# A lower pace for the weight loads, logits turned ahead of the expert products, and a new opening list

## The chip, the cores and the metric

One core of a Trainium2 chip. The time is device microseconds for one execution of the whole program, as the median of a few runs. The names of the engines are those of the profile: PE (TensorE matmuls, with PEld for its weight loads), DVE (VectorE), ACT (ScalarE), POOL (GpSimd) and SP (SyncE, which here issues almost all the DMAs).

## What is computed

A banded attention, a soft mixture of experts and a two-layer FFN with tanh-shrink, one behind the other, all in float32. Cut to what matters:

```python
# attention: 4 batches, 8 heads, 512 local and 32 global positions, head size 64
out_g = sm(scale * q_g @ k_all.T) @ v_all            # the global rows see everything
s_ll  = where(|i - j| <= 32, scale * q_l @ k_l.T, -1e9)
out_l = sm(concat(scale * q_l @ k_g.T, s_ll)) @ concat(v_g, v_l)
x = concat(out_g, out_l)                             # 2304 tokens x 512

# soft mixture of 8 experts with 4 slots each
logits = x @ phi                                     # 2304 x 32
d = softmax of logits over the tokens;  c = softmax of logits over the slots
slot_out[e] = relu((d.T @ x)[e] @ w1[e]) @ w2[e]     # 512 -> 1024 -> 512
x = c @ slot_out

# FFN
h = x @ w_in;  g = h - tanh(h);  out = g @ w_out     # 512 -> 2048 -> 512
```

## The kernel before

The program is scheduled by hand: the order in which the code calls an engine's operations is the order in which that engine runs them. It has four stages.

**Attention** (to about 126 us of the profiled execution) runs 33 iterations over pieces of the sequence. PE computes scores, transposes and products with the values, DVE and ACT the softmax, POOL spreads q and k and rolls v. Meanwhile SP loads the next q, k and v, and also prefetches what later stages need: the expert weights, in pieces of 512 KB that go to free buffers called slot (and later to buffers of attention as they come free: k_w, v_w, q, pg), and the FFN's w_in. How many go in an iteration is set by one line in the loop:

```python
while queued < LEAD + PACE * it:
```

`queued` counts the KB of everything loaded so far, so that an iteration with few loads of its own gets more weights. Behind the last iteration the weights go out as fast as buffers come free and the DMA queue takes them. All of this stands at line 124, a helper. At most a handful of loads are under way at a time: before it issues the next, SP waits for an older one.

**The hand-over** (to about 137 us) ends the softmax over the tokens and forms the slots' inputs. Line 906 turns a column of maxima, 854 turns the slots' inputs into the PSUM bank `sit`, and DVE's 930 copies it to the two halves of `siT`, on which the expert products rest. Three small DVE operations behind it (`d3["sums"]`, line 399; 935; `make_irep`, 828) prepare the sums by which the expert outputs are scaled.

**The expert stage** (to about 171.5 us) runs 16 units, `UNITS`, each an expert's W1 (line 1026) or W2 (line 1065) in two halves. In between stand the transposes of the hidden layer (1049) and the combine weights, c, in five pieces, of 4, 4, 4, 4 and 1 tiles of 128 tokens: `combine(4 * k, ..)` turns the logits `lT` (lines 972 and 974) and computes a softmax on DVE and ACT, and `combine_turn` turns the result back (998) and casts it into place (ACT, 1000 and 1011). `CPREP` and `CTURN` say behind which units these stand. The stage's last work is the conversion of w_out's first chunk from a 64-bit form: head (ACT, 562), shift, high and low (DVE, 566, 571, 576), whi (ACT, 1091) and wlo (POOL, 1092).

**The FFN** follows. Its beginning is written out as a list of words, `OPENING`, that are called one by one: `sos` scales and copies the experts' outputs (ACT, 1312), `turn` and `soT` transpose them (1318), `m0`, `rows`, `ms`, `parts`, `mhi` and `mlo` form the product of the experts' outputs with w_in block by block (1327, 1140, 1154, 1158, 1162), `head`, `S`, `H`, `L`, `whi` and `wlo` convert the chunks of w_out. `h:i:part` is the hidden product of step i (1197), `sq`, `t0`, `t1`, `hi` and `lo` its activation and its split into a high and a low half (ACT 1201, DVE 1207 and 1211, ACT 1219, POOL 1223), and `T:i:j` three products of 512 columns (1236, 1237, 1238) into the accumulator of tile j; the third needs `lo`. From step 9 a loop does the same in a fixed pattern, up to about 382 us.

`keep_warm(bank, n)` (line 674) is a product of n columns whose result nobody reads; one of 256 columns stands before ahead of `sos`.

Of the kernel before, what the change touches and what calls it, by code (L numbers as in the profile page):

```python
# [12 lines left out]
ALU = mybir.AluOpType  # L13
# [5 lines left out]
NT = 17  # L19
NE = 8  # L20
WARM = 3
LEAD, PACE = 2700, 1200
KEEP = 2
SPK = 1
C0 = 4
# [24 lines left out]

PHASES = [(0, 6, 0, 8), (6, 6, 0, 8), (12, 5, 0, 8), (0, 6, 8, 16), (6, 6, 8, 16), (12, 5, 8, 16)]
OPENING = """
    sos:0 turn:0 sos:1 turn:1 turn:2 head:1 S:1 turn:3 soT:1 H:1 L:1 soT:0 m0:0 head:2 m0:1 m0:2 m0:3 mhi:0 mlo:0
    rows:1 ms:1 S:2 whi:1 wlo:1 h:0:2 sq:0:2 h:0:3 t0:0:2 t1:0:2 h:0:1 sq:0:3 t0:0:3 t1:0:3 sq:0:1 parts:1 mhi:1
    rows:2 hi:0:2 lo:0:2 T:0:0 mlo:1 h:1:0 ms:2 parts:2 h:1:1 t0:0:1 t1:0:1 hi:0:3 lo:0:3 T:0:1 T:0:2 sq:1:0 t0:1:0
    t1:1:0 hi:0:1 lo:0:1 mhi:2 mlo:2 sq:1:1 hi:1:0 head:3 h:2:0 sq:2:0 t0:1:1 t1:1:1 hi:1:1 S:3 T:0:3 T:0:4 H:2
    h:2:1 sq:2:1 T:0:5 lo:1:0 T:1:0 T:1:1 lo:1:1 t0:2:0 t1:2:0 hi:2:0 lo:2:0 h:3:0 sq:3:0 L:2 whi:2 wlo:2 T:1:3
    T:1:2 H:3 T:1:5 t0:2:1 t1:2:1 hi:2:1 lo:2:1 h:3:1 sq:3:1 T:1:4 t0:3:0 t1:3:0 T:2:1 T:2:4 t0:3:1 head:4 S:4
    T:2:2 hi:3:0 lo:3:0 t1:3:1 hi:3:1 lo:3:1 h:4:0 h:4:1 sq:4:0 L:3 whi:3 wlo:3 t0:4:0 t1:4:0 T:2:3 T:2:5 sq:4:1
    t0:4:1 T:2:0 H:4 hi:4:0 lo:4:0 h:5:0 sq:5:0 T:3:2 T:3:0 head:5 t1:4:1 h:5:1 hi:4:1 lo:4:1 sq:5:1 L:4 whi:4  # L60
    wlo:4 t0:5:1 S:5 T:3:5 T:3:4 t1:5:1 hi:5:1 lo:5:1 T:3:3 T:3:1 head:6 T:4:4 t0:5:0 t1:5:0 h:6:0 sq:6:0 hi:5:0
    lo:5:0 h:6:1 sq:6:1 H:5 L:5 whi:5 wlo:5 head:7 t0:6:0 t0:6:1 T:4:2 T:4:1 T:4:5 t1:6:0 hi:6:0 lo:6:0 T:4:3 T:4:0
    T:5:3 t1:6:1 hi:6:1 lo:6:1 S:6 H:6 L:6 T:5:4 h:7:0 sq:7:0 t0:7:0 t1:7:0 h:7:1 T:5:0 T:5:2 whi:6 T:5:1 T:5:5
    sq:7:1 t0:7:1 t1:7:1 hi:7:1 h:8:0 sq:8:0 hi:7:0 S:7 H:7 L:7 wlo:6 T:6:0 head:24 T:6:1 T:6:3 T:6:4 T:6:2 h:8:1
    whi:7 lo:7:0 T:6:5 wlo:7 head:25 t0:8:0 t1:8:0 h:9:0 hi:8:0 lo:8:0 sq:8:1 t0:8:1 sq:9:0 t0:9:0 t1:9:0 T:7:0
    keep:0 T:7:2 keep:2 lo:7:1 t1:8:1 T:7:3 keep:3 hi:8:1 lo:8:1 T:7:1 keep:1 S:24 S:25 H:25 T:7:4 keep:4 h:9:1
    sq:9:1 t0:9:1 h:10:0 sq:10:0 T:7:5 T:8:3 hi:9:0 lo:9:0 T:8:1 keep:5 T:8:4 T:8:5 t0:10:0 t1:10:0 hi:10:0 T:8:0
    H:24 t1:9:1 hi:9:1 lo:9:1 L:24 T:8:2 h:10:1 sq:10:1 t0:10:1 t1:10:1 lo:10:0 L:25 hi:10:1 lo:10:1 h:11:0 sq:11:0
"""
LOOP = 9  # L70
SOON = 23
# [11 lines left out]
def band_attention_soft_moe_tanhshrink_kernel(  # L83
# [589 lines left out]
    def keep_warm(bank, n):  # L673
        T.matmul(bank[:, 0:n], lhsT=ident, rhs=win[0][:, 0:n], skip_group_check=True)

    with tc.manual_schedule():
# [252 lines left out]
        for g in range(2):  # L929
# [1 line left out]
                out=diagonal(siT[g][:, :, 16 * g:], 128, 4, 32),  # L931
                in_=sit[:, 0:128].rearrange("p (k g e s) -> p g k e s", k=4, g=2, e=4)[:, g],
            )
        d3["sums"]()
        V.tensor_tensor(out=rr, in0=mrun[:, 2:3], in1=f, op=ALU.mult)
        make_irep()

        es_pa.close()

        free.insert(0, once)  # L940
# [4 lines left out]
        def bank(j):  # L945
            return psa.tile([128, 512], F32, tag=f"a{j}", name=f"a{j}")
# [19 lines left out]

        c4_t = {}

        def combine(t0, n):
            lps = bank(4)  # L970
            if n == 4:
                T.transpose(lps[:, 0:128], lT[:, t0 // 4, :], ident)
            else:
                T.transpose(lps[:, 0:32], lT[0:32, 4, :], ident[0:32, 0:32])
            l = lps[:, 0:32 * n].rearrange("p (i s) -> p i s", i=n)
            cc = wk.tile([128, 128], F32, tag="E", name="cc", bufs=1)[:, 0:32 * n].rearrange("p (i s) -> p i s", i=n)
            cm = wk.tile([128, 4], F32, tag="mb", name="cm")[:, 0:n]
# [117 lines left out]
        for u, (m, e) in enumerate(UNITS):  # L1095
            for hf in range(2):
                (emit_W2 if m else emit_W1)(e, hf)
                release(4 * u + 2 * hf)
                if hf == 0:
                    more([], u > 1)  # L1100
            if m == 0 and e in (2, 4):
                room_hr(e // 4)
            if u == 1:
                row_sums()
            if u in TURNS:
                turn_h(TURNS.index(u))
            if u == CVAT:
                cv.append(slot()[0].bitcast(I32).rearrange("p (a f) -> p a f", a=2))
            if u == 5:
                cst_t.extend(slot(True)[0].bitcast(F32R) for _ in range(3))  # L1110
            k = CTURN.index(u) if u in CTURN else None
            if k is not None:
                combine_turn(4 * k, 4 if k < 4 else 1)
            k = CPREP.index(u) if u in CPREP else None
            if k is not None:
                combine(4 * k, 4 if k < 4 else 1)
            more([], u > 1)
            while len(w_sl) == len(wq) and len(free) > 4 and len(LATE) - len(late) < EARLY:
                load_late()
# [436 lines left out]
```

## Time and profile before

| | us |
|---|---|
| median of 3 runs (lowest, highest) | 398.27 (398.13, 399.73) |
| the profiled execution | 396.89 |
| its span, from the first to the last instruction | 395.0 |
| PE busy in it | 375.2 (95%) |
| DVE, ACT, POOL busy | 272.3, 218.8, 210.0 |
| DMA, moved | 70.43 MB |

The span lies within the profiled execution's own time; the difference is start and end. The rows further down come from that one execution. Times are in microseconds from the start of its span. A timeline row gives the start of a group of instructions, how long it was busy, the engine, the line of the kernel, the operation with what it writes and reads, and in brackets the idle time just before and what ended it. The mean granted clock of TensorE was 0.999 of full speed.

### The profile page before, as it was taken

Reading aid. Unit: us, or ns where it says so; the run is one execution under the profiler, and the core shown is the slowest. Engines: PE = TensorE matmul, PEld = TensorE weight load, DVE = VectorE, ACT = ScalarE, POOL = GpSimd, SP = SyncE. Lnnn points to the kernel's source line nnn. Section 1 sums busy time; section 2 is a strip of 40 time slices with the busy share of each in tenths; the row PEclk is TensorE's granted clock in tenths of the full one; section 3 lists DMA queues with packets and bytes.
Section 4 is the critical chain, followed back from the end, with each engine's and each line's share of the span. In section 5 each row is a group of like instructions: output and inputs, shape, how many; then the busy total and the mean of one; then the engine's idle time right before and its main releaser. Section 6 shows DMA issues by size and latency. Waiting matters only on the chain.

```text
span 395.0 us, 10202 instructions
## 1 busy us (share of the span) xinstructions
PE 375.2 (95%) x3764; PEld 281.0 (71%) x3764; DVE 272.3 (69%) x836; ACT 218.8 (55%) x544; POOL 210.0 (53%) x276
## 2 busy tenths in 40 slices
PE   7879889999989899999999999999999999999994
PEld 3768667777778433346888887786878888888873
DVE  4577778796566545469997697788798996546451
ACT  2667765876666303167668544766666464345430
POOL 2667575775564010025976544457666586457441
PEclk9999999999999999999999999999999999999999
DMA  7899998999968999998312012032000013004004
GB/s 183 258 401 302 336 352 266 367 333 305 338 200 251 335 368 418 416 419 333 100 50 58 0 54 55 6 100 56 0 2 2 0 45 116 0 2 157 4 2 141
DMA packets 33978, 70.43 MB, mean 178 GB/s; under 512 B 3840, under 2 KB 10752, under 8 KB 33920
## 3 DMA queue, kind: packets, MB, share of 16 engines
q1 hardware_dynamic: 33776, 69.56, 51.3%
q8 instruction: 32, 0.52, 0.5%
q14 instruction: 26, 0.21, 0.2%
q10 hardware_dynamic: 144, 0.13, 0.1%
HBM read 65.22 MB, written 4.46 MB: 176 GB/s over the span
## 4 chain that ended last, share of the span: by engine, by line
PE 72%; POOL 9%; DMA 7%; issue 7%; DVE 2%; SPq 1%; ACT 1%; DVEq 0%; POOLq 0%; ACTq 0%
PE a L1238 14%; PE a L1237 13%; PE a L1236 13%; PE sc L268 7%; PE h L1197 4%; POOL slot L1223 3%; PE a L1026 3%; PE X L301 3%; PE ptp L289 3%; POOL q L230 3%; DMA slot<-in_w_dram 3%; PE gsc L461 2%; DMA slot<-in_w_out_dram 2%; POOL v L230 2%; POOL k L230 1%
## 5 line engine op out<-in xcount | busy, mean ns | idle before, releaser
L1223 POOL TENSOR_TENSOR slot<-slot 128x384 fp32r<-128x384 f32 (+2 forms) x97 | 100.0, 1034 | 81.0 <-ACT slot L1219 75.7
L1238 PE MATMUL a<-slot 128*128 128x512 f32 x272 | 107.8, 396 | 0.1
L1236 PE MATMUL a<-slot 128*128 128x512 f32 x272 | 106.9, 393 | 0.3 <-ACT slot L1219 0.3
L1237 PE MATMUL a<-slot 128*128 128x512 f32 x272 | 107.1, 394 | 0.0
L1207 DVE SCALAR_TENSOR_TENSOR h<-slot,h 128x384 f32<-128x384 f32 (+1 forms) x96 | 51.0, 533 | 38.1 <-ACT slot L1201 37.8
L1219 ACT CAST slot<-slot 128x384 fp32r<-128x384 f32 (+2 forms) x97 | 47.7, 493 | 42.5 <-DVE slot L1211 42.1
L1201 ACT ACTIVATE slot<-h 128x384 f32<-128x384 f32 (+1 forms) x96 | 44.8, 470 | 36.6 <-PE h L1197 36.0
L1236 PEld LDWEIGHTS a<-slot 128*128 128x128 f32 x272 | 51.1, 188 | 13.4 <-ACT slot L1219 1.5
L1238 PEld LDWEIGHTS a<-slot 128*128 128x128 f32 x272 | 51.0, 188 | 12.2 <-POOL slot L1223 0.8
L1237 PEld LDWEIGHTS a<-slot 128*128 128x128 f32 x272 | 51.0, 188 | 8.6 <-POOL slot L1092 0.2
L1211 DVE TENSOR_TENSOR slot<-slot,h 128x384 f32<-128x384 f32 (+1 forms) x96 | 50.3, 526 | 8.7 <-POOL slot L1223 1.3
L278 ACT ACTIVATE sm<-sm,mb 128x128 f32<-128x128 f32 x128 | 41.2, 395 | 17.5 <-DVE mb L274 17.2
L268 PE MATMUL sc<-k,q 128*64 128x128 f32 x512 | 39.1, 294 | 4.7 <-POOL q L230 3.1
L230 POOL TENSOR_SCALAR v<-v 32x1300 f32<-32x1300 f32 (+5 forms) x40 | 33.3, 833 | 14.3 <-PE xgp L506 11.0
L268 PEld LDWEIGHTS sc<-k,q 128*64 128x64 f32 x512 | 33.3, 208 | 10.5 <-POOL q L230 5.0
L230 POOL TENSOR_SCALAR q<-q 64x256 f32<-64x256 f32 x62 | 28.0, 452 | 18.5 <-issue 6.5
L1092 POOL TENSOR_TENSOR slot<-k_w,slot 128x512 fp32r<-128x512 f32 x16 | 20.9, 1305 | 28.3 <-ACT slot L1091 28.0
L274 DVE CUSTOM_DVE_ANT_0 sm<-sc,mask 128x128 f32<-128x128 f32 x128 | 30.0, 284 | 4.6 <-PE sc L268 2.9
L1197 PE MATMUL h<-slot 128*128 128x384 f32 x94 | 31.3, 342 | 0.1
L301 PE MATMUL X<-v,pt 128*32 128x65 f32 x1024 | 23.1, 223 | 2.4 <-issue 2.4
L1197 PEld LDWEIGHTS h<-slot 128*128 128x128 f32 x94 | 17.6, 188 | 7.9 <-DVE slot L1211 2.3
L301 PEld LDWEIGHTS X<-v,pt 128*32 128x32 f32 x1024 | 17.0, 109 | 7.1 <-issue 6.1
(261 smaller groups left out, 523.9 us busy)
## 6 DMA issues: line engine op xcount, KB each, us to landing
slot<-in_w_dram SPq DMA_DIRECT2D x54, 512.0 KB, 7.7
slot<-in_w_in_dram SPq DMA_DIRECT2D x16, 256.0 KB, 6.7
slot<-in_w_out_dram SPq DMA_DIRECT2D x8, 512.0 KB, 9.8
k<-in_k_dram SPq DMA_DIRECT2D x7, 576.0 KB, 7.9
q<-in_q_dram SPq DMA_DIRECT2D x15, 256.0 KB, 5.9
out_dram<-o SPq DMA_DIRECT2D x15, 256.0 KB, 2.3
v<-in_v_dram SPq DMA_DIRECT2D x8, 390.0 KB, 5.0
slot<-in_w_in_dram SPq DMA_DIRECT2D x6, 512.0 KB, 9.8
```

The lines of the kernel that those rows point to most:

```text
L230: G.tensor_scalar(out=o, in0=i, scalar1=0.0, scalar2=1.0, op0=ALU.add, op1=ALU.mult)
L268: T.matmul(sc[64 * i:64 * i + 64, a, :], lhsT=q_b[2][:, 256 * i + jj:256 * i + 256:4], rhs=k[:, i, :, WINDOWS[t][jj][0]], skip_group_check ...
L301: T.matmul(X[32 * jj:32 * jj + 32, h, :], lhsT=pt[:, 128 * jj + 32 * h:128 * jj + 32 * h + 32], rhs=v[:, WINDOWS[t][jj][0], 65 * h:65 * h ...
L1197: T.matmul(u_t[i, part][0], lhsT=mst(128 * fc, 128), rhs=cst(128 * t0 + c.start, n))
L1201: S.activation(out=u, in_=h, func=AF.Square)
L1207: V.scalar_tensor_tensor(out=h, in0=u, scalar=-2.5, in1=h, op0=ALU.add, op1=ALU.mult)
L1211: V.tensor_tensor(out=g, in0=u, in1=h, op=ALU.mult)
L1219: S.copy(out=ghi, in_=g)
L1223: G.tensor_tensor(out=glo, in0=g, in1=ghi.bitcast(F32), op=ALU.subtract)
L1236: T.matmul(acc_t[j], lhsT=ghi[:, c], rhs=whi[fc], start=first, stop=False)
L1237: T.matmul(acc_t[j], lhsT=ghi[:, c], rhs=wlo[fc], start=False, stop=False)
L1238: T.matmul(acc_t[j], lhsT=glo[:, c], rhs=whi[fc], start=False, stop=last)
```

## The change

Four things are changed. `PACE` falls from 1,200 to 1,060, so that fewer weights go out in an iteration of attention. Two products nobody reads, of 256 and 192 columns, stand ahead of the turn of the maxima and the turn of `sit`. The combine's logits are turned all at once ahead of W1, four pieces into the bank of `a4` (that `sit` has been in) and the small piece into a bank of `h`, and stay there; the three small DVE operations go behind the first half of the first W1. And the pieces of the combine come in another order: `(CPREP.index(u) - 1) % 5` takes the small one first, so that the last turn, behind unit 13, is now that of a piece of 4 tiles. The opening list is written anew.

```diff
-LEAD, PACE = 2700, 1200
+LEAD, PACE = 2700, 1060
...
-    sos:0 turn:0 sos:1 turn:1 turn:2 head:1 S:1 turn:3 soT:1 H:1 L:1 soT:0 m0:0 head:2 m0:1 m0:2 m0:3 mhi:0 mlo:0
-    rows:1 ms:1 S:2 whi:1 wlo:1 h:0:2 sq:0:2 h:0:3 t0:0:2 t1:0:2 h:0:1 sq:0:3 t0:0:3 t1:0:3 sq:0:1 parts:1 mhi:1
-    rows:2 hi:0:2 lo:0:2 T:0:0 mlo:1 h:1:0 ms:2 parts:2 h:1:1 t0:0:1 t1:0:1 hi:0:3 lo:0:3 T:0:1 T:0:2 sq:1:0 t0:1:0
...
+    sos:0 turn:0 sos:1 head:1 S:1 turn:1 soT:0 turn:2 turn:3 soT:1 m0:0 m0:1 m0:2 H:1 L:1 head:2 m0:3 mhi:0 mlo:0
+    whi:1 wlo:1 rows:1 ms:1 h:0:2 sq:0:2 h:0:3 sq:0:3 h:0:1 parts:1 rows:2 sq:0:1 t0:0:2 t1:0:2 hi:0:2 lo:0:2 T:0:0
+    t0:0:3 t1:0:3 mhi:1 mlo:1 h:1:0 h:1:1 ms:2 parts:2 t0:0:1 hi:0:3 lo:0:3 T:0:2 T:0:1 S:2 t1:0:1 sq:1:0 t0:1:0
...
+        keep_warm(mp[:, 128:], 256)
         T.transpose(mp[0:1, 0:128], mcur, ident)
...
+        keep_warm(mp[:, 256:], 192)
         turn_si(sit, (0, 1))
...
-        d3["sums"]()
-        V.tensor_tensor(out=rr, in0=mrun[:, 2:3], in1=f, op=ALU.mult)
-        make_irep()
-
         es_pa.close()
...
+        lps, lpg = bank(4), hbank()[:, 0:32]
+        T.transpose(lpg, lT[0:32, 4, :], ident[0:32, 0:32])
+        for b in range(4):
+            T.transpose(lps[:, 128 * b:128 * b + 128], lT[:, b, :], ident)
+
         def combine(t0, n):
-            lps = bank(4)
-            if n == 4:
-                T.transpose(lps[:, 0:128], lT[:, t0 // 4, :], ident)
-            else:
-                T.transpose(lps[:, 0:32], lT[0:32, 4, :], ident[0:32, 0:32])
-            l = lps[:, 0:32 * n].rearrange("p (i s) -> p i s", i=n)
+            l = (lps[:, 32 * t0:32 * t0 + 128] if n == 4 else lpg).rearrange("p (i s) -> p i s", i=n)
...
                 (emit_W2 if m else emit_W1)(e, hf)
+                if u == 0 and hf == 0:
+                    d3["sums"]()
+                    V.tensor_tensor(out=rr, in0=mrun[:, 2:3], in1=f, op=ALU.mult)
+                    make_irep()
...
-            k = CTURN.index(u) if u in CTURN else None
+            k = (CTURN.index(u) - 1) % 5 if u in CTURN else None
...
-            k = CPREP.index(u) if u in CPREP else None
+            k = (CPREP.index(u) - 1) % 5 if u in CPREP else None
```

Below, rows of the order in which an engine runs its instructions: line, operation, what it writes and reads, shape, how many in a row. The lines of the changed kernel are counted anew, so that 1024 is W1 and 1209 and 1213 are the two tail steps.

SP, the loads of the last iterations of attention and those behind them (`slot<-in_w_dram` is a piece of 512 KB of expert weights):

```order
 L124 DMA phi_g<-in_phi_dram 128x128
 L124 DMA v<-in_v_dram 96x520
-L124 DMA k_w<-in_w_dram 128x2x512
+L124 DMA slot<-in_w_dram 128x2x512 x5
 L124 DMA q<-in_w_dram 128x512
 L124 DMA pg<-in_w_dram 128x512
 L124 DMA k_w<-in_w_dram 128x512
 L124 DMA v_w<-in_w_dram 128x512
+L124 DMA k_w<-in_w_dram 128x1024
```

Five pieces that stood among the loads of earlier iterations stand here now, ahead of the loads to buffers of attention, one of which moves back by four places.

PE at the hand-over to W1, before (`mask_92` and `siacc` are the slots' inputs, `a` the banks of the expert products):

```order
L838 MATMUL mp<-ident,mrow 32x1 x4
L423 MATMUL ps<-x,e 32x256 x4
L854 MATMUL sit<-mask_92,siacc 128x32 x4
L1026 MATMUL a_2829<-slot,siT 32x512 x4
L1026 MATMUL a_2838<-slot,siT 32x512 x4
```

The same place now:

```order
L838 MATMUL mp<-ident,mrow 32x1 x4
L423 MATMUL ps<-x,e 32x256 x4
L674 MATMUL mp<-win_100,ident 128x192
L854 MATMUL sit<-mask_92,siacc 128x32 x4
L968 MATMUL h<-ident,lT 128x32
L970 MATMUL a_2828<-ident,lT 128x128 x4
L1024 MATMUL a_2835<-slot,siT 32x512 x4
L1024 MATMUL a_2847<-slot,siT 32x512 x4
```

One product nobody reads stands ahead of the turn of `sit`, and the five transposes of the logits between it and W1; among the W1 and W2 products none of these is left.

DVE in the opening, before (`k_w` is the chunk of w_out in conversion, L566 its shift, L1207 and L1211 the tails of the FFN's first step):

```order
L1162 TENSOR_TENSOR slot<-a_3211,slot 64x128
L233 COPY ms<-a_3219 128x384
L566 TENSOR_SCALAR k_w<-k_w 128x512
L1207 SCALAR_TENSOR_TENSOR h<-slot,h 128x128
L1211 TENSOR_TENSOR slot<-slot,h 128x128
L1207 SCALAR_TENSOR_TENSOR h<-slot,h 128x256
L1211 TENSOR_TENSOR slot<-slot,h 128x256
L1162 TENSOR_TENSOR slot<-a_3243,slot 64x384
```

The same place now:

```order
L1164 TENSOR_TENSOR slot<-a_3208,slot 64x128
L233 COPY ms<-a_3220 128x384
L1209 SCALAR_TENSOR_TENSOR h<-slot,h 128x128
L1213 TENSOR_TENSOR slot<-slot,h 128x128
L1209 SCALAR_TENSOR_TENSOR h<-slot,h 128x256
L1213 TENSOR_TENSOR slot<-slot,h 128x256
L1164 TENSOR_TENSOR slot<-a_3235,slot 64x384
L1209 SCALAR_TENSOR_TENSOR a_3233<-slot,a_3233 128x384
L566 TENSOR_SCALAR k_w<-k_w 128x512
L1213 TENSOR_TENSOR slot<-slot,a_3233 128x384
```

The shift of w_out's third chunk has gone behind the first tail step of part 1.

## Rows read from the trace of the kernel before

**Rows 1.** Stretches: busy us by engine (instructions), PEclk, DMA share, GB/s.

```profile
20.00:104.00 84.00, 76.83 (x1642) 62.50 (x1643) 62.01 (x312) 60.29 (x169) 55.82 (x102) 1.00 1.00 334
104.00:124.00 20.00, 18.97 (x433) 15.32 (x433) 12.85 (x77) 12.62 (x39) 11.05 (x22) 1.00 0.72 222
132.00:140.00 8.00, 6.95 (x70) 3.24 (x70) 3.15 (x13) 0.88 (x6) 0.53 (x1) 1.00 0.99 342
140.00:172.00 32.00, 31.92 (x274) 11.17 (x266) 16.08 (x63) 7.36 (x27) 2.40 (x3) 1.00 1.02 408
172.00:180.00 8.00, 7.49 (x43) 3.99 (x43) 6.68 (x14) 5.42 (x15) 3.22 (x4) 1.00 1.03 420
180.00:380.00 200.00, 199.91 (x890) 161.24 (x889) 152.73 (x272) 115.45 (x249) 122.07 (x113) 1.00 0.15 52
```

**Rows 2.** PE's waits, 15 to 130 us: line waited for, us, times, longest.

```profile
PE X L301 <- issue: 2.4, 4, 1.0
PE sc L268 <- POOL q L230: 2.0, 3, 1.1
```

**Rows 3.** Timeline of POOL: start, us, instruction, idle before and releaser.

```profile
19.12 0.88 POOL L230 TENSOR_SCALAR q<-q 64x256 f32<-64x256 f32 x2 [1.91 <-DMA q<-in_q_dram]
```

**Rows 4.** Expert loads issued 155 to 161 us: durations, first and last start, landing.

```profile
L124 SPq DMA_DIRECT2D slot<-in_w_dram x4: 327/328/328, 155.9 to 159.5; - x4
...
DMA to landing us min/median/max: 9.9/10.2/10.3
```

**Rows 5.** Timeline of PE at the hand-over to W1.

```profile
132.00 0.27 PE L906 MATMUL mp<-ident,mrun 128*1 128x128 f32 x1 [0.64 <-DVE mrun L384]
...
135.19 1.08 PE L854 MATMUL sit<-mask,siacc 128*128 128x32 f32 x8 [0.42 <-DVE mask L922]
136.87 3.64 PE L1026 MATMUL a<-slot,siT 128*32 128x512 f32 x32 [0.61 <-DVE mrun L399]
...
142.61 0.33 PE L972 MATMUL a<-ident,lT 128*128 128x128 f32 x1
142.87 1.06 PE L1026 MATMUL a<-slot,siT 128*32 128x512 f32 x8
```

**Rows 6.** Timeline of PE, last expert units and behind them.

```profile
165.19 0.66 PE L998 MATMUL h<-ident,c 128*128 128x128 f32 x4
165.77 1.93 PE L1065 MATMUL a<-slot 128*32 128x512 f32 x16
167.63 0.33 PE L998 MATMUL h<-ident,c 128*128 128x128 f32 x1
167.88 3.64 PE L1065 MATMUL a<-slot 128*32 128x512 f32 x32
171.46 0.70 PE L674 MATMUL a<-win,ident 128*128 128x256 f32 x2
```

**Rows 7.** Timeline of DVE, the copies to siT.

```profile
136.37 0.36 DVE L930 COPY siT<-sit 128x64 f32<-128x64 f32 x2 [0.85 <-PE sit L854]
```

**Rows 8.** Timeline of ACT from the combine's casts to sos.

```profile
165.88 0.71 ACT L1011 CAST slot<-h 128x192 fp32r<-128x192 f32 x3 [3.48 <-PE h L998]
167.99 0.27 ACT L1000 CAST slot<-h 128x128 fp32r<-128x128 f32 x1 [1.40 <-PE h L998]
...
170.80 0.62 ACT L1091 CAST slot<-k_w 128x512 fp32r<-128x512 f32 x1 [1.95 <-DVE k_w L576]
171.59 0.84 ACT L1312 ACTIVATE sos<-a,mrun 128x256 f32<-128x256 f32 x2 [0.18 <-PE a L1065]
```

**Rows 9.** Timeline of PE, the first FFN product.

```profile
178.30 0.50 PE L1236 MATMUL a<-slot 128*128 128x512 f32 x1 [0.31 <-ACT slot L1219]
```

**Rows 10.** Timelines of DVE (two rows) and POOL (one row) in the opening.

```profile
173.03 0.43 DVE L566 TENSOR_SCALAR k_w<-k_w 128x512 int32<-128x512 int32 x1 [2.26 <-ACT k_w L562]
...
176.06 1.33 DVE L566 TENSOR_SCALAR k_w<-k_w 128x512 int32<-128x512 int32 x1
...
175.84 1.27 POOL L1092 TENSOR_TENSOR slot<-k_w,slot 128x512 fp32r<-128x512 f32 x1 [3.07 <-ACT slot L1091]
```

More of the change, by code (lines that the diff above doesn't have):

```diff
@@ L52 @@
 OPENING = """
-    sos:0 turn:0 sos:1 turn:1 turn:2 head:1 S:1 turn:3 soT:1 H:1 L:1 soT:0 m0:0 head:2 m0:1 m0:2 m0:3 mhi:0 mlo:0
-    rows:1 ms:1 S:2 whi:1 wlo:1 h:0:2 sq:0:2 h:0:3 t0:0:2 t1:0:2 h:0:1 sq:0:3 t0:0:3 t1:0:3 sq:0:1 parts:1 mhi:1
-    rows:2 hi:0:2 lo:0:2 T:0:0 mlo:1 h:1:0 ms:2 parts:2 h:1:1 t0:0:1 t1:0:1 hi:0:3 lo:0:3 T:0:1 T:0:2 sq:1:0 t0:1:0
-    t1:1:0 hi:0:1 lo:0:1 mhi:2 mlo:2 sq:1:1 hi:1:0 head:3 h:2:0 sq:2:0 t0:1:1 t1:1:1 hi:1:1 S:3 T:0:3 T:0:4 H:2
-    h:2:1 sq:2:1 T:0:5 lo:1:0 T:1:0 T:1:1 lo:1:1 t0:2:0 t1:2:0 hi:2:0 lo:2:0 h:3:0 sq:3:0 L:2 whi:2 wlo:2 T:1:3
@@ L58 @@
[L58 to L67, printed above, removed]
@@ L68 @@
-    H:24 t1:9:1 hi:9:1 lo:9:1 L:24 T:8:2 h:10:1 sq:10:1 t0:10:1 t1:10:1 lo:10:0 L:25 hi:10:1 lo:10:1 h:11:0 sq:11:0
+    sos:0 turn:0 sos:1 head:1 S:1 turn:1 soT:0 turn:2 turn:3 soT:1 m0:0 m0:1 m0:2 H:1 L:1 head:2 m0:3 mhi:0 mlo:0
+    whi:1 wlo:1 rows:1 ms:1 h:0:2 sq:0:2 h:0:3 sq:0:3 h:0:1 parts:1 rows:2 sq:0:1 t0:0:2 t1:0:2 hi:0:2 lo:0:2 T:0:0
+    t0:0:3 t1:0:3 mhi:1 mlo:1 h:1:0 h:1:1 ms:2 parts:2 t0:0:1 hi:0:3 lo:0:3 T:0:2 T:0:1 S:2 t1:0:1 sq:1:0 t0:1:0
+    t1:1:0 hi:0:1 lo:0:1 T:0:5 sq:1:1 t0:1:1 t1:1:1 mhi:2 mlo:2 hi:1:0 lo:1:0 head:3 S:3 h:2:0 sq:2:0 T:0:3 hi:1:1
@@ new lines @@
+    lo:1:1 T:0:4 H:2 t0:2:0 t1:2:0 hi:2:0 lo:2:0 h:2:1 sq:2:1 T:1:0 T:1:1 L:2 whi:2 wlo:2 h:3:0 sq:3:0 T:1:3 H:3
+    t0:2:1 t1:2:1 hi:2:1 lo:2:1 T:1:5 t0:3:0 t1:3:0 T:1:2 h:3:1 sq:3:1 t0:3:1 head:4 S:4 t1:3:1 hi:3:0 T:1:4 T:2:1
+    h:4:0 sq:4:0 T:2:2 lo:3:0 hi:3:1 lo:3:1 L:3 whi:3 wlo:3 T:2:4 h:4:1 sq:4:1 T:2:0 T:2:3 T:2:5 t0:4:0 t1:4:0
+    hi:4:0 lo:4:0 h:5:0 sq:5:0 t0:4:1 head:5 T:3:0 T:3:2 H:4 t1:4:1 hi:4:1 lo:4:1 L:4 h:5:1 sq:5:1 t0:5:1 T:3:1
+    T:3:4 whi:4 wlo:4 T:3:5 T:3:3 S:5 t1:5:1 hi:5:1 t0:5:0 t1:5:0 T:4:4 H:5 head:6 lo:5:1 h:6:0 h:6:1 sq:6:0 T:4:0
@@ new lines @@
+    L:5 T:4:2 hi:5:0 T:4:3 T:4:5 lo:5:0 t0:6:0 sq:6:1 t0:6:1 whi:5 T:4:1 t1:6:0 h:7:0 t1:6:1 h:7:1 wlo:5 T:5:1
+    T:5:5 hi:6:1 lo:6:1 hi:6:0 lo:6:0 sq:7:0 T:5:4 head:7 T:5:2 T:5:0 S:6 H:6 L:6 whi:6 wlo:6 t0:7:0 t1:7:0 sq:7:1
+    T:5:3 t0:7:1 t1:7:1 hi:7:1 S:7 H:7 L:7 h:8:0 sq:8:0 T:6:1 T:6:0 hi:7:0 lo:7:0 whi:7 wlo:7 T:6:3 T:6:4 T:6:5
+    head:24 head:25 lo:7:1 t0:8:0 t1:8:0 hi:8:0 lo:8:0 T:6:2 h:8:1 sq:8:1 h:9:0 sq:9:0 t0:9:0 t0:8:1 t1:8:1 S:24
+    T:7:0 keep:0 T:7:2 keep:2 T:7:3 keep:3 T:7:1 keep:1 t1:9:0 T:7:4 hi:8:1 T:7:5 keep:4 S:25 H:25 h:9:1 sq:9:1
@@ L69 @@
+    h:10:0 sq:10:0 t0:10:0 t0:9:1 hi:9:0 T:8:1 keep:5 T:8:2 H:24 lo:8:1 T:8:3 T:8:5 T:8:4 t1:9:1 hi:9:1 lo:9:0
+    t1:10:0 hi:10:0 L:24 lo:9:1 T:8:0 h:10:1 sq:10:1 t0:10:1 t1:10:1 hi:10:1 L:25 lo:10:0 lo:10:1 h:11:0 sq:11:0
 """
```

## The prediction

> **What bounds the kernel now.** I read the busy table by stretch first [rows 1], then the list of what PE waits for during attention [rows 2], then the loads and the timelines at the places that the diff touches [rows 3 to 10]. From 180 us to 380 us PE is busy for 199.9 of 200 us [rows 1]: the FFN products run back to back, the diff leaves their number as it is, and no order of the other engines' work can bring anything there. From 140 to 172 us, the expert products, PE is busy for 31.92 of 32 us, and the DMA engines are full too (1.02, 408 GB/s), so there two resources end together. Slack is left in three places: attention (76.83 of 84 us from 20 to 104, 18.97 of 20 behind it), the hand-over to W1 (132 to 140: 6.95 of 8) and the opening (172 to 180: 7.49 of 8). The granted clock is 1.00 in every one of these stretches, the higher of the two levels, 2.4 GHz.
>
> **Part 1, the weights at 1,060 units an iteration.** In the order of SP five loads of 512 KB leave the stream of attention, one each from five places, and stand together behind the last v load, in the stretch from 104 to 124 us. To shorten attention they would have to hold PE up now. The list of PE's waits over attention has none on a DMA; its two largest lines are 2.4 us in four stalls in which the profile sees no releaser, and 2.0 us in three waits for POOL's q [rows 2]. The DMA engines are full from 20 to 104 us (1.00) [rows 1], and POOL does wait for a q load once, 1.91 us before 19.12 [rows 3]. PE's waits for q are POOL's work coming late, in which no load is named. I cost the gain in attention at nothing; the end on the good side is the whole 2.0 us.
>
> The other side is where the five loads go. In 140 to 172 us loads land every 1.2 us: four issues of 512 KB from 155.9 to 159.5 us, each (159.5 - 155.9) / 3 = 1.2 us behind the one before, are on their way for 9.9 to 10.3 us [rows 4]. Five cost 5 x 1.2 = 6.0 us of the DMA engines. What is idle: from 104 to 124 us the engines are 0.72 busy, so 0.28 x 20 = 5.6 us [rows 1]. Everything behind comes 0.4 us later, if the hole is filled. The last expert load is issued at 159.5 and lands 10.2 us later, at 169.7 [rows 4]; PE takes it for the last quarter of the 32 products that begin at 167.88 and end at 171.46 [rows 6], at 167.88 + 0.75 x 3.58 = 170.57. That is 0.87 us of slack, of which part 2 takes 0.45: 0.42 us are left against 0.4 us. Cost: 0. If the hole isn't filled it costs up to the second rival.
>
> **Part 2, the logits turned ahead of W1.** Five transposes leave the expert stage. One shows its price as the distance to the next matmul: 142.61 to 142.87 = 0.26 us [rows 5]. Read in the same way the other four cost 0.20 three times and, for the 32 wide one, 0.17: 0.26 + 3 x 0.20 + 0.17 = 1.03 us. In front of W1 four of them stand in a row: four transposes of this size in a row took 165.77 - 165.19 = 0.58 us [rows 6]. They write the bank that sit was in, and so wait for both copies to siT just as W1's first product does; these run from 136.37 for 0.36 us [rows 7] and W1 starts at 136.87, so the 0.58 us are added behind that wait and not hidden in it. The fifth, 32 columns wide, has the wait (0.61 us) for itself: 0. Net 0.58 - 1.03 = -0.45 us at the end of W2. The ends: -1.03 if the four should fall into the wait after all, and 0.58 - 5 x 0.145 = -0.15 if single ones really cost what they do in a row. I take -0.45, by the rows of the very instructions.
>
> The three DVE operations that move behind the first half of W1 (sums, rr, the copy for irep) keep their order on DVE, and their last result, irep, goes to PE only behind the first unit of W1: 0.
>
> **The warming products.** 256 columns go in front of the product at 132.00, which waits 0.64 us, and 192 columns in front of the turn of sit, which waits 0.42 us [rows 5]. Two products of 256 columns in a row took 0.70 us [rows 6], one so about 0.35, and one of 192 less. The first is covered; the second too, if it is let go when the 0.42 us begin. Should it come late, half of it, 0.2 us, would stick out. The granted clock is 1.00 there without them [rows 1], so they have nothing to win. 0, ends 0 and +0.2.
>
> **Part 3, the combine's own order.** The turn behind unit 13 now has four transposes and three casts where it had one and one; the turn behind unit 6 has one where it had four. PE reaches the turn behind unit 13 at 167.63 - 0.45 - (0.58 - 0.25) = 166.85 [rows 6]. Casts begin 165.88 - 165.19 = 0.69 us behind the transposes and take 0.71 [rows 8]: they end at 166.85 + 0.69 + 0.71 = 168.25, against 167.99 + 0.27 = 168.26 now. So the head of w_out's first chunk on ACT, DVE's three steps on it and the cast at 170.80, which all stand behind these casts, don't move, and ACT is free for sos at 170.80 + 0.62 = 171.42. Now sos starts at 171.59, having waited 0.18 us for PE's last product [rows 8]. **Of PE's 0.45 us, sos gets the 0.18 us that it waited, and no more**: then the chain of casts is what comes last. I take -0.1, since a cast more on ACT may cost the rest.
>
> **Part 4, the opening list.** The first FFN product starts at 178.30, 0.31 us after PE has finished a block of row sums, at 177.99 [rows 9]. It waits for ACT's cast, that for DVE's two tail steps, and these stand on DVE behind a shift for w_out's third chunk, which took 1.33 us from 176.06 [rows 10]; its twin at 173.03 took 0.43. Now the shift stands behind the tails of the first two parts. Without it the tails could start at about 176.1 instead of 177.4, and the cast would be there a microsecond sooner: PE comes last, and the gain is its 0.31 us, no more. -0.3, ends -0.5 (all that PE idles from 172 to 180 us, 8 - 7.49) and the third rival.
>
> Why did that shift take 1.33 us? It ran beside POOL's subtraction from 175.84, which took 1.27 us [rows 10]. The Trainium skill ("SBUF — State Buffer", section "SBUF: two separate sides") says that VectorE and GpSimd share a port pair as an exclusive lock: whoever starts first holds it for the whole instruction. The row agrees (0.43 alone, 1.33 beside POOL). By that rule the moved shift is a danger where it goes: it now stands close to POOL's subtractions for the first parts, and the third rival is what that would do.
>
> **Sum.** 0 (attention) + 0 (warming) - 0.1 (hand-over to sos) - 0.3 (opening) = -0.4 us. Behind 180 us nothing can give it back or add to it. The profiled execution took 396.89 us, its span 395.0; it would be 396.5. The median of the runs shown is 398.27, 1.4 above that execution, so the forecast for the median is 398.27 - 0.4 = 397.9.
>
> **Rivals.** What a measurement can tell from no change is about 0.5%, 2.0 us here: faster is under 396.28, slower over 400.26.
>
> First: **the loads did hold attention up.** For it: DMA at 1.00 for 84 us, POOL's wait of 1.91 us for q [rows 3], and 9% of the bytes gone from this stretch (5 x 0.5 MB of 334 GB/s x 84 us = 28 MB); also, PE idles 7.2 us in the 84 us with full engines, 1.7 in 20, and 1.0 in the 20 us in which they are 0.72 busy [rows 1]. Against it: no wait of PE names a DMA, and the stalls without releaser are not put down to a load either [rows 2]. If all of PE's waits for POOL's q go, 397.9 - 2.0 = 395.9. Chance 0.20.
>
> Second, on the other side: **the hole isn't filled and the last expert weights come late.** Where the loads behind the five wait for buffers that come free at fixed times, half the hole (2.8 us) stays empty: lateness 6.0 - 2.8 = 3.2 us, less 0.42 us of slack, less the 0.35 us by which PE now ends ahead of sos: +2.4 us: 397.9 + 2.4 = 400.3. It decides from a lateness of 0.8 us on. Engines at 1.02 all the way to W2's end speak for it, since nothing can be caught up there [rows 1]; the 0.28 that is idle speaks against it. Chance 0.11.
>
> Third: **the opening gives its gain back.** The shift, held up once more to 1.33 us, stands ahead of the second tail step of part 1, whose cast and subtraction feed PE's fourth to sixth product groups: 0.9 us later, of which PE covers 0.3: 398.27 - 0.1 + 0.6 - 0.3 = 398.5. Chance 0.14, still no change by measurement.
>
> My forecast, 397.9, has 0.55, and with it go 396.9 to 398.9. Faster 0.20, same 0.69, slower 0.11. The range of 8 in 10 reaches from nearly the first rival to the third and beyond: 395.8 to 399.3.
>
> **What would show it.** Attention: W1's first product at 136.9 + 0.6 us, PE's waits for POOL unchanged; a start of W1 by 1 us earlier is the first rival. Loads: no PE wait on a DMA from 160 to 172 us; one of over 0.5 us is the second. PE's last W2 product 0.45 us earlier against W1's start less 0.58, yet sos at most 0.2 us earlier, now waiting for nothing. Opening: the tails at about 176.3, first FFN product without idle time before it, and 0.43 us for the moved shift; 1.3 us there, with PE idle at 181 us, is the third. I am wrong if PE's start of W1 moves by over 1 us, or if idle time turns up behind 180 us.

## The result and the profile after

The changed kernel took 395.28 us as the median of 12 executions, the kernel before 398.31 of 12: the ratio is 0.9913, with a 95% interval of 0.9888 to 0.9938, 3.0 us less by the medians and 3.5 by the ratio. That is below the range that was forecast (395.8 to 399.3). Two more measurements, each beside the kernel before on its own chip, gave 0.9971 (0.9943 to 0.9998) and 0.9939 (0.9910 to 0.9969). The mean of the three is 0.994, 2.3 us less. The intervals of the first two don't meet (0.9938 and 0.9943): measurements of one kernel differ by more than their intervals say. Single executions of either kernel differ by several microseconds (392.7 to 398.3 for the changed kernel in the first measurement), and the one that was profiled was the longest of its twelve: 398.32 us with a span of 396.5, longer than the profiled execution of before (396.89, 395.0). So its trace can't be read by its end. Of its 1.5 us, W1's later start makes 1.8 (0.56 of it by the change, as shown below) and the end behind the last group of FFN products 1.0, while the stages between save 1.3. That end takes 6.1 to 7.3 us over all 20 traces, 6.2 in the trace of before and 7.3 in this one. So the trace is read stage by stage, and the start of W1 by many traces.

The changed kernel by stretches, columns as in [rows 1]:

```profile
20.00:104.00 84.00, 76.48 (x1621) 62.22 (x1613) 61.42 (x311) 59.81 (x169) 55.60 (x101) 0.98 0.93 302
104.00:124.00 20.00, 18.95 (x459) 15.52 (x459) 12.75 (x72) 12.97 (x39) 11.64 (x24) 1.00 0.92 323
132.00:140.00 8.00, 7.34 (x70) 3.83 (x67) 3.97 (x17) 1.35 (x9) 0.53 (x1) 1.00 0.92 292
140.00:172.00 32.00, 31.92 (x281) 11.02 (x275) 15.66 (x63) 6.23 (x24) 1.90 (x2) 1.00 1.03 416
172.00:180.00 8.00, 7.81 (x49) 4.01 (x44) 5.46 (x13) 6.07 (x15) 3.01 (x3) 1.00 1.03 421
180.00:380.00 200.00, 199.91 (x890) 161.12 (x889) 153.89 (x274) 115.82 (x250) 123.31 (x114) 1.00 0.17 56
```

The loads have moved as the order said: the DMA share fell from 1.00 to 0.93 in the first row and rose from 0.72 to 0.92 in the second. The FFN is as full as before.

PE of the changed kernel at the hand-over and at the end of W2 (start, busy, line, idle before it):

```profile
133.24 0.27 PE L907 MATMUL mp<-ident,mrun 128*1 128x128 f32 x1 [0.20 <-DVE mrun L384]
...
136.44 1.08 PE L854 MATMUL sit<-mask,siacc 128*128 128x32 f32 x8
...
138.12 0.63 PE L970 MATMUL a<-ident,lT 128*128 128x128 f32 x4 [0.43 <-DVE mrun L399]
138.68 3.64 PE L1024 MATMUL a<-slot,siT 128*32 128x512 f32 x32
...
168.79 4.02 PE L1063 MATMUL a<-slot 128*32 128x512 f32 x32
172.74 0.70 PE L674 MATMUL a<-win,ident 128*128 128x256 f32 x2
```

Against [rows 5]: from the turn of the maxima to the turn of sit 3.20 us (3.19 before), so the warming products took nothing. From there to W1 2.24 us instead of 1.68: the four transposes stand behind the wait and cost 0.56. Against [rows 6]: from W1's first product to the end of W2 34.06 us instead of 34.59. The last 32 products took 4.02 us instead of 3.64: the last eight of them no longer start at the pace of the others, and one of PE's weight loads among them, at 171.76, has waited 0.25 us for a DMA. That late weights make all of the 0.38 us is likely and not shown, since PE's weight loads have such waits also where these products take 3.64 us (changed_third). In four runs below with the logits turned ahead (changed_third, no_warm, opening_undone, turns_alone) W1 to the end of W2 took 33.7 to 33.8 us.

ACT of the changed kernel, the casts behind unit 13, the cast of the first chunk of w_out and sos:

```profile
168.90 0.71 ACT L1009 CAST slot<-h 128x192 fp32r<-128x192 f32 x3 [1.73 <-PE h L996]
...
172.15 0.62 ACT L1089 CAST slot<-k_w 128x512 fp32r<-128x512 f32 x1 [1.95 <-DVE k_w L576]
172.86 0.84 ACT L1314 ACTIVATE sos<-a,mrun 128x256 f32<-128x256 f32 x2
```

From W1 to sos it is 34.18 us, 34.72 before [rows 8]; with the 0.56 in front of W1 sos comes 0.02 us later. In the four runs named it was 34.0 to 34.1 us, so that sos came 0.1 to 0.2 us earlier.

The opening: DVE's first tail and the moved shift,

```profile
177.43 0.30 DVE L1209 SCALAR_TENSOR_TENSOR h<-slot,h 128x128 f32<-128x128 f32 x1
...
180.06 0.43 DVE L566 TENSOR_SCALAR k_w<-k_w 128x512 int32<-128x512 int32 x1
```

PE's first FFN product,

```profile
179.19 0.50 PE L1238 MATMUL a<-slot 128*128 128x512 f32 x1
```

and POOL's first two subtractions for the FFN:

```profile
178.46 0.46 POOL L1225 TENSOR_TENSOR slot<-slot 128x128 fp32r<-128x128 f32 x1
180.29 0.78 POOL L1225 TENSOR_TENSOR slot<-slot 128x256 fp32r<-128x256 f32 x1 [1.38 <-ACT slot L1221]
```

The first FFN product has no idle time ahead of it any more [rows 9], and comes 6.45 us behind the end of W2 instead of 6.84. The moved shift takes 0.43 us in its new place instead of 1.33 [rows 10]: it starts 0.23 us ahead of POOL's next subtraction, which takes 0.78 us (0.72 for the same one before).

One saving more lies behind it. The first products of all FFN groups, kernel before and changed kernel (count, ns least/median/most, first and last start):

```profile
L1236 PE MATMUL a<-slot x272: 387/392/501, 178.3 to 388.8; 128*128 128x512 f32 x136
```

```profile
L1238 PE MATMUL a<-slot x272: 387/392/795, 179.2 to 389.3; 128*128 128x512 f32 x136
```

From the first to the last it is 210.5 us before and 210.1 after. In five traces of kernels with the old list it was 210.48 to 210.54, in fifteen with the new one 210.06 to 210.32.

### The profile page after: what moved, and what is told of

The parts are those of the page before. It is cut to its first block, busy times and chain, and to the rows that moved or that the text cites. A ratio compares the mean times of both kernels' runs of the same rounds, so it can differ in the third digit from the quotient of the medians.

```text
span 396.5 us, 10214 instructions
## 1 busy us (share of the span) xinstructions
PE 376.3 (95%) x3768; PEld 282.4 (71%) x3768; DVE 271.9 (69%) x836; ACT 219.1 (55%) x544; POOL 210.8 (53%) x276
## 4 chain that ended last, share of the span: by engine, by line
## 5 line engine op out<-in xcount | busy, mean ns | idle before, releaser
L230 POOL TENSOR_SCALAR v<-v 32x1300 f32<-32x1300 f32 (+5 forms) x40 | 33.5, 839 | 18.1 <-PE xgp L506 15.0
L301 PE MATMUL X<-v,pt 128*32 128x65 f32 x1024 | 22.0, 223 | 1.8 <-issue 1.8
L289 PE MATMUL ptp<-ident,sm 128*128 128x128 f32 x128 | 21.5, 291 | 0.7 <-ACT pt L291 0.7
```

The costliest lines, as they stand in the source:

```text
L230: G.tensor_scalar(out=o, in0=i, scalar1=0.0, scalar2=1.0, op0=ALU.add, op1=ALU.mult)
```

## The experiments

Ratios are to the kernel before on the same chip, with 95% intervals; 0.0025 is 1 us.

**Each part alone.**

p1060_alone, and the same kernel again as p1060_again:

```diff
-LEAD, PACE = 2700, 1200
+LEAD, PACE = 2700, 1060
```

> The kernel before with one number changed, 1,060 instead of 1,200. Theory A (the loads held attention up, and the lower pace is most of the 3 us): 395.5 to 396.5 us, and in its trace fewer or shorter stalls of PE in attention, W1 starting at about 135. Theory B (the gain lies behind attention, in the turned-ahead logits, their order and the opening): 398.3, as before, W1 at about 137.

> The kernel before with pace 1,060 alone, a second time. If the pace carries the gain that the forecast missed: 1.0 to 2.0 us under the kernel before. If not: within 0.6 us of it.

0.9968 (0.9935 to 1.0001), then 0.9997 (0.9971 to 1.0023): 396.92 and 397.12 us. The mean is 0.7 us less, and neither is clear of no change. W1 starts at 136.7 in the first trace and at 133.8 in the second.

opening_alone, and the same again as opening_again, the kernel before with the new list of words:

```diff
-    sos:0 turn:0 sos:1 turn:1 turn:2 head:1 S:1 turn:3 soT:1 H:1 L:1 soT:0 m0:0 head:2 m0:1 m0:2 m0:3 mhi:0 mlo:0
...
+    sos:0 turn:0 sos:1 head:1 S:1 turn:1 soT:0 turn:2 turn:3 soT:1 m0:0 m0:1 m0:2 H:1 L:1 head:2 m0:3 mhi:0 mlo:0
...
```

> The kernel before with the new opening list alone. Theory A: 397.8 to 398.3 (at most 0.5 us, all that PE idled from 172 to 180 us). Theory B: 396.5 to 397.5.

> The kernel before with the new opening list alone, a second time. If the list is worth what the traces show between W2 and the first FFN product: 0.2 to 0.6 us under the kernel before. If its first result was its size: 1.2 to 1.8 us under.

0.9961 (0.9928 to 0.9993) and 0.9971 (0.9943 to 0.9999), 397.34 and 396.46 us: the first ratio is 1.6 us, the second 1.2, both above the 0.5 us of idle time that I had allowed for. Their traces show 0.38 us less between W2's end and the first FFN product (6.46 against 6.84) and 0.33 from there to the last product (210.18 against 210.51), 0.7 us, within both intervals. What lies between 0.7 and the measured 1.2 to 1.6 the traces don't show, and the intervals don't demand it.

turns_alone, the changed kernel without its pace, its list and its warming products:

```diff
-LEAD, PACE = 2700, 1060
+LEAD, PACE = 2700, 1200
...
-        keep_warm(mp[:, 128:], 256)
...
-        keep_warm(mp[:, 256:], 192)
```

> The kernel before with the logits turned ahead of W1, the combine's new order and the three small DVE operations moved, but with pace 1,200, the old opening list and without the two warming products. Theory A: 398.0 to 398.3 (0.45 us gained by PE at the end of W2, of which sos gets 0.1 to 0.2). Theory B: 396.5 to 397.5.

0.9995 (0.9963 to 1.0027), 398.54 us: nothing that the total could show. In its trace W1 to sos takes 34.05 us against 34.72, with 0.56 in front: 0.1 us, as forecast for sos.

no_warm, the changed kernel without the two lines `keep_warm`:

> The changed kernel without the two warming products. If they do nothing, as the granted clock of 1.00 at that place in the kernel before says: the same as the changed kernel within 0.5 us, and W1 no later against the turn of the maxima. If they hold the clock: 0.5 to 2 us slower, with a granted clock under 1.00 between 132 and 145 us.

0.9955 (0.9926 to 0.9983), 396.10 us, beside 0.9971 for the changed kernel measured with it, so no slower without them. From the turn of the maxima to the turn of sit 3.19 us, and the granted clock is 1.00 in the stretches 124 to 132, 132 to 140 and 140 to 172 us: the products do nothing in this pair. But one of the eight traces without them, that of opening_again, has a granted clock of 0.62 from 136 to 140 us, and W1's first 32 products take 5.34 us instead of 3.64:

```profile
136.46 5.34 PE L1026 MATMUL a<-slot,siT 128*32 128x512 f32 x32 [0.61 <-DVE mrun L399]
```

PE's waits ahead of it are those of the trace of before (0.64, 0.43 and 0.61 us). None of the twelve traces with the products has this. One against none is too few to say that the products prevent it, or that they do nothing.

**The changed kernel again, and with one part undone.**

after_again and changed_third are the changed kernel itself:

> The changed kernel itself once more, for the size of the gain and a second trace. If the 3 us of the first measurement are its size: 395.0 to 395.7. If part of it was the spread between executions (a gain of 0.9 us behind W1 and 1 us of the pace): 396.0 to 396.8. In its trace the stretch from W1's first product to the first FFN product takes 40.5 us either way; only the start of W1 differs.

> The changed kernel a third time. If the pace is worth about 1 us and the opening list 0.7 us, the rest nothing: 1.5 to 2.2 us under the kernel before of the same chip.

0.9971 (396.89 us) and 0.9939 (395.54 us), as told above.

p1200_undone, later p1200_undone_again beside changed_third, has its pace set back:

```diff
-LEAD, PACE = 2700, 1060
+LEAD, PACE = 2700, 1200
```

> The changed kernel with the pace set back to 1,200, all else as changed. Theory A: 397.3 to 398.0, nearly all of the gain gone. Theory B: 395.3 to 395.8, as the changed kernel.

> The changed kernel with pace 1,200, a second time. If the pace is worth about 1 us: 0.6 to 1.4 us above the changed kernel of the same call, and 0.5 to 1.0 under the kernel before. If the pace is nothing at these two values: within 0.4 us of the changed kernel.

0.9955 (0.9925 to 0.9986), then 0.9984 (0.9961 to 1.0006). The second, at 397.62 us beside 395.54 on the same chip, is 2.1 us above the changed kernel. The first had no changed kernel beside it: 0.9955 lies between the changed kernel's 0.9913 and 0.9971, and its 396.51 us between the two theories, so it decides nothing.

opening_undone has the old list:

> The changed kernel with the old opening list. From the traces (0.4 us between the end of W2 and the first FFN product): 0.4 us over the changed kernel, 396.6 to 397.2 if that is at 396.2 to 396.8. If the list is worth the 1.5 us that the list alone measured: 397.7 to 398.3.

0.9981 (0.9943 to 1.0018), 396.35 us, below both expectations, and too wide to tell 0.4 from 1.5.

pace_opening, the kernel before with pace and list alone:

> The kernel before with pace 1,060 and the new opening list, without the turned-ahead logits, their order and the warming products. If these are worth nothing in the total, as their own run says (0.0 us) and as 0.58 us ahead of W1 against 0.53 us behind it say: as the changed kernel, 396.0 to 397.0. If they matter together with the others: 397 to 398.

0.9954 (0.9920 to 0.9987), 396.45 us: the level of the changed kernel (0.994) without the turned-ahead logits and the warming products.

Taken together by their ratios: the five measurements with the lower pace and the new list (the changed kernel three times, no_warm, pace_opening) average 0.9946, 2.1 us less; the four with the list at pace 1,200 0.9968, 1.3 us; the three with the lower pace and the old list 0.9982, 0.7 us; the one with neither 0.9995, 0.2 us. The differences give the list 1.1 to 1.4 us and the pace 0.5 to 0.9. With single intervals of 1.2 us to either side such a difference is known to about 0.8 us at best, so the pace is not clear of zero. The list is, by its own two measurements and by every trace.

old_turns, the changed kernel with the pieces of the combine in their old order:

```diff
-            k = (CTURN.index(u) - 1) % 5 if u in CTURN else None
+            k = CTURN.index(u) if u in CTURN else None
...
-            k = (CPREP.index(u) - 1) % 5 if u in CPREP else None
+            k = CPREP.index(u) if u in CPREP else None
```

> The changed kernel with the combine's pieces in their old order: the single tile's turn last, behind unit 13, as before. If the chain of casts ahead of sos is what comes last there: sos starts up to 0.3 us earlier against the end of W2, the total 0.1 to 0.3 us faster than the changed kernel or equal. If the order is worth something by itself: slower by over 0.5 us.

0.9972 (0.9936 to 1.0007), 397.02 us; the total says nothing, but the trace does. PE's waits from 135 to 182 us (line waited for, us, times, longest):

```profile
PE h L1047 <- DVE hc L1048: 1.0, 2, 0.5
PE h L996 <- DVE hc L1048: 0.5, 1, 0.5
```

Both my expectations were wrong: sos did not come earlier against the end of W2, and the expert stage took 35.59 us instead of 34.06, by three waits that no other trace here has. The turned-ahead small piece of the logits sits in one of the two banks of h until its softmax has read it. In the old order that is behind unit 10, so the transposes of the hidden layer have one bank and wait for DVE each time. The new order, small piece first, is what makes turning ahead free.

**The pace as a dose.** Five kernels differ from the changed one in the number alone: 3,000, 1,400, 1,130, 1,020, 980.

> The changed kernel with pace 3,000: the weights go out as early as buffers allow. Theory A (loads that come too early hold attention's own loads up, through POOL): slower than the changed kernel by 1.5 to 4 us, 397 to 399.5, with POOL's waits for q and qg longer than in any trace so far. Theory B (attention doesn't feel the weights): the same as the changed kernel within 0.6 us.

> The changed kernel with pace 1,400. Theory A (the loads hold attention up by degrees, through POOL and through PE's instruction stalls): 1.5 to 4 us slower than the changed kernel, 398 to 400, with POOL's waits for q and qg over 10 us and a later W1. Theory B (only the extreme pace of 3,000 does that, 1,060 against 1,200 is nothing): within 0.6 us of the changed kernel.

> The changed kernel with pace 1,130. Loads hold attention up by degrees: 0.3 to 1 us slower than the changed kernel, between it and pace 1,200. If nothing happens between 1,060 and 1,200: the same within 0.5 us.

> The changed kernel with pace 1,020. At 980 the last weights came 5.8 us late while W1 came 1 to 2 us earlier. If that cost begins right under 1,060: W1 to the end of W2 takes 36 to 38 us instead of 34.1, and the total is 0.5 to 3 us above the changed kernel. If it begins only under 1,020: 34.1 us, and the total is equal or 0.5 us less.

> The changed kernel with pace 980, lower still. Theory A: 0.3 to 1 us faster than the changed kernel in attention, unless the loads put off come late at the end of W2 (then PE waits on a DMA there in the trace, and it is slower by that). Theory B: the same as the changed kernel, or slower by that wait.

| pace | us | ratio (95%) | W1 starts | POOL waits for DMA | PE stalls, no releaser | W1 to end of W2 |
|---|---|---|---|---|---|---|
| 3,000 | 415.97 | 1.0422 (1.0388 to 1.0455) | 155.5 | 33.5 | 1.2 | 34.3 |
| 1,400 | 403.28 | 1.0140 (1.0085 to 1.0195) | 140.2 | 19.4 | 2.8 | 34.5 |
| 1,200 | (6 traces) | | 137.8 (136.5 to 138.7) | 7.2 | 5.4 (4.8 to 6.4) | 34.8 (33.8 to 36.3) |
| 1,130 | 397.62 | 1.0007 (0.9978 to 1.0036) | 136.2 | 4.2 | 4.4 | 34.6 |
| 1,060 | (9 traces) | | 136.9 (133.8 to 139.5) | 4.7 | 4.3 (1.0 to 7.7) | 34.4 (33.7 to 35.6) |
| 1,020 | 398.31 | 1.0003 (0.9972 to 1.0035) | 136.7 | 2.3 | 4.1 | 36.4 |
| 980 | 401.86 | 1.0085 (1.0055 to 1.0114) | 135.5 | 6.7 | 4.2 | 40.4 |

Times in us, the waits and stalls as sums up to 130 us of the trace; the rows of 1,200 and 1,060 are means over all traces with that pace (least and most in brackets), and 0.56 is taken off W1 where the logits are turned ahead of it. The last column mixes kernels with and without the turned logits; its 36.3 holds the fall of the clock in opening_again, its 35.6 the three waits of old_turns. Both ends show. Above 1,200 the loads of the weights hold attention up, at 1,400 in PE's own waits (the first two rows of the waits for a DMA up to 130 us that are not ACT's):

```profile
POOL k L230 <- DMA qg<-in_qg_dram: 17.2, 6, 3.6
...
PE gsc L461 <- DMA k<-in_k_dram: 4.7, 3, 1.8
```

and at 3,000 in one wait of 12.2 us:

```profile
PE gsc L461 <- DMA k<-in_k_dram: 12.2, 1, 12.2
```

At both, the totals are further up than I had expected (398 to 400 and 397 to 399.5).

At 980 the weights come late, and the total is 0.85% up. PE at the end of W2 at pace 1,020, where it begins to show:

```profile
171.48 1.05 PE L1063 MATMUL a<-slot 128*32 128x512 f32 x4 [0.17 <-DMA slot<-in_w_dram]
172.72 1.05 PE L1063 MATMUL a<-slot 128*32 128x512 f32 x4 [0.19 <-DMA slot<-in_w_dram]
173.70 0.70 PE L674 MATMUL a<-win,ident 128*128 128x256 f32 x2
```

The last pieces of W2 arrive 1.24 us apart, and PE goes at that pace. But a single trace doesn't place the kink: that of p1200_undone has the same two waits at pace 1,200, with 35.6 us from W1 to the end of W2. And 1,130 and 1,020 measured as the kernel before, although both have the new list, and 1,130 as expected by neither theory. The kernel before itself had a median of 397.46 us beside them and of 398.19 in another measurement on that chip, so 0.7 us of this is spread. Between 1,200 and 980 the starts of W1 (135.5 to 137.8) lie within what traces of one pace differ by (133.8 to 139.5): the table has no slope to show there.

## Why the prediction was wrong

**What stood.** Behind the start of W1 most steps are as forecast, place by place: 0.56 us for the four transposes (0.58 forecast), sos all but unmoved against the hand-over (-0.1 forecast, +0.02 in the trace, -0.1 to -0.2 in four others), the warming products nothing between the turn of the maxima and that of sit, the first FFN product without idle time ahead of it, the moved shift at 0.43 us and not 1.33, so that the third rival did not come. The hole took the loads in (0.92 busy, 0.72 before). The weights' lateness, for which I had 0.42 us of slack against 0.4, was a little more than that in this trace: the last group of products takes 4.02 us instead of 3.64, and sos waits for it, 0.18 us later against W1 than in changed_third. The second rival came at pace 980, not here.

**The term that was mis-sized: the opening, -0.3 us.** It is -0.7 in the traces, and more in the totals (1.1 to 1.4). I counted what the shift in front of DVE's tails costs the first product and stopped there. The same 1.33 us on DVE also held up the next operation of another chain: the low half of the second block of the hidden product's weights (L1162), at 178.74 in the trace of before,

```profile
178.74 0.56 DVE L1162 TENSOR_TENSOR slot<-a,slot 64x384 fp32r<-64x384 f32 x1
179.33 0.56 DVE L1207 SCALAR_TENSOR_TENSOR a<-slot,a 128x384 f32<-128x384 f32 x1
```

ends at 179.30, and PE's next hidden product starts at 179.36, 0.26 us later than the product ahead of it lets it (products of this kind follow each other by 0.23 us, 178.87 + 0.23 = 179.10). In the changed kernel that hidden product follows its predecessor at once, at 179.99 behind 179.76.

```profile
178.87 0.47 PE L1238 MATMUL a<-slot 128*128 128x512 f32 x1
179.36 0.45 PE L1197 MATMUL h<-slot 128*128 128x384 f32 x1
```

```profile
179.76 0.40 PE L1240 MATMUL a<-slot 128*128 128x512 f32 x1
179.99 0.52 PE L1199 MATMUL h<-slot 128*128 128x384 f32 x2
```

The sentence that nothing behind 180 us could add to it, from a PE that is busy for 199.9 of 200 us, was wrong by 0.33 us, of which this gap is 0.26: the gap lies under the modelled end of the product ahead (178.87 + 0.47 = 179.34), and so counts as busy.

**The step that failed: attention at nothing.** I reasoned that PE's list of waits has none on a DMA, so thinner loads could not shorten attention, and gave the opposite a chance of 0.20 as the first rival. The dose shows that attention's length does hang on the pace from 1,200 up (W1 at 137.8, 140.2 and 155.5). At 1,060 against 1,200 W1 starts 0.9 us earlier on average (136.9 over nine traces, 137.8 over six), but with a standard error of 0.7 us, and the totals give the pace 0.5 to 0.9 us, not clear of zero: that the step missed a gain is likely and not shown. What is shown is that its reason was wrong. It is not the rival's mechanism either: PE's waits for POOL's q are the same at both (2.9 and 2.8 us), although POOL's own waits for loads fall from 7.2 to 4.7. The difference lies in the stalls for which the profile names no releaser, 5.4 against 4.3 us. I had taken "no releaser" for "not the DMA", and had read only the largest line of them [rows 2]. The list goes on with three more of them, and together they are 5.1 of the 8.1 us that PE waits from 15 to 130 us:

```profile
PE xgp L506 <- issue: 1.2, 1, 1.2
PE ps L368 <- issue: 0.9, 1, 0.9
...
PE gsc L461 <- issue: 0.6, 1, 0.6
```

Here is one of them, in the trace of before, PE at 103.16:

```profile
103.16 0.22 PE L301 MATMUL X<-v,pt 128*32 128x65 f32 x1 [0.97 <-issue]
```

and the DMA queues of the same trace from 100.5 to 101.9 us (packets, MB, share of the engines):

```profile
q1 hardware_dynamic: 318, 0.53, 100.8%
q8 instruction: 1, 0.02, 4.5%
```

One packet of instructions of 16 KB, from 100.7 to 101.7 us, among 318 of loads on full engines, and PE goes on 1.5 us after its end. The 20 traces have 64 such stalls of 0.5 us or more up to 130 us, and every one ends 1.2 to 1.7 us behind the end of an instruction packet, although such stretches cover only 8% of the time (trace of before, 20 to 125 us). So PE waits for its own program there, and the program comes over the engines that the weights keep full. These stalls also go with the spread between executions: over the 15 traces at 1,060 and 1,200 W1 starts at 133.8 where they sum to 2.8 us (p1060_again) and at 139.5 where they sum to 7.7 (opening_undone), with a correlation of 0.77. It fits the means that thinner loads make these stalls shorter, but a packet takes as long on idle engines as on full ones (trace of before: 0.92 to 1.38 us behind 200 us, at a DMA share of 0.12, and 0.96 to 1.54 from 20 to 104 us, at 1.00), and whether loads delay its start no trace shows. Moreover, single traces with one pace differ by more (1.0 to 7.7 us) than the means do, and at 1,400 and 3,000, where PE waits for loads outright, the stalls are shorter. So this part is not shown, and what thinner loads change in attention stays open.

**The sum.** The traces give 0.7 us for the list, the totals 0.5 to 0.9 for the pace: 1.2 to 1.6. By the totals alone, with 1.1 to 1.4 for the list, it is about 2. The three measurements average 2.3 with single ones from 1.2 to 3.5; the first, which the forecast is held against, is the largest, and about 1 us of it has no cause here but the spread. The range was too narrow on that side for two reasons: the first rival had its price capped at 2.0 us, all of a wait that then did not move, and nothing was added for the spread of a median of executions that differ by several microseconds, which the three runs shown (398.13 to 399.73) beside a profiled one of 396.89 already told.

## What to carry to other kernels

A stall without a releaser is not a stall without a cause: look for instruction packets just ahead of it, and don't count a transfer as hidden because no wait names it. An operation that blocks an in-order engine delays everything that queues behind it; follow each of these to its reader, not only the one on the critical path. And where two costs meet (loads too early, weights too late), move the one number by steps on both sides, with several measurements of each: here 1,400 and 980 were clearly worse, and between them single measurements could not tell.

## What the runs showed of the hardware

The granted clock fell during attention in 10 of the 20 traces, in three of them only in its first 12 us, in seven later, among them that of the changed kernel. There it stood for 8 us at

```profile
20.00:24.00 4.00, 2.01 (x34) 1.77 (x24) 1.62 (x9) 1.60 (x5) 1.39 (x3) 0.79 1.05 395
24.00:28.00 4.00, 4.00 (x64) 3.29 (x61) 1.90 (x13) 3.06 (x7) 3.16 (x5) 0.78 0.94 347
```

(columns as in [rows 1]), that is in part at the lower of the two levels, 1.2 GHz. By the rows it cost 1.4 us: PE takes 3.58 us for three groups behind the stall (22.45 to 26.03) that take 2.18 in the trace of before (21.05 to 23.23). Just ahead of it PE had stalled for 1.99 us without a releaser, the longest stall of that trace:

```profile
22.17 0.36 PE L506 MATMUL xgp<-v,pg 128*32 128x65 f32 x7 [1.99 <-issue]
```

In the trace of before, whose stalls were 1.22 us at the most, the clock stayed at 1.00 through attention. So this stall cost 3.4 us instead of 2.0. In five of the seven traces the fall stands behind such a stall, of 1.79 to 2.15 us. Not each one does this: 1.88 us in the trace of p1060_alone and 2.87 us in that of opening_undone, the longest of all, were followed by no fall.

```profile
55.56 0.24 PE L301 MATMUL X<-v,pt 128*32 128x65 f32 x1 [2.87 <-issue]
```

Stalls and falls are both part of why executions of one kernel differ. The Trainium skill ("TensorE: Matmul & The Clock Gate", section "What's actually happening") has these two levels and an idle array falling to the lower one; the row agrees.

The Trainium skill's exclusive lock ("SBUF — State Buffer", section "SBUF: two separate sides") agreed once more: the same shift took 1.33 us beside POOL's subtraction and 0.43 us where it started ahead of the subtraction.
